# Strassen's algorithm, one level, in the last product of a fused attention, mixture and channel-mixing kernel

## The chip, the cores and the metric

One core of a Trainium2 chip runs the whole program in one launch. The metric is device time in microseconds. The core has five engines with a queue of instructions each: TensorE (matmuls, with weight loads beside them), VectorE, ScalarE, GpSimd and SyncE, which here only issues DMAs.

## The reference

Three layers follow one another, on 8 sequences of 576 tokens (4608 in all), in float32.

- Linear attention with 8 heads of 64: features exp(p) and exp(-p) of the projected queries and keys, a key-value sum per head, a division.
- A mixture of four causal attention experts, the two best per token weighted by a softmax.
- A channel-mixing layer:

```
xk = mu_k * x + (1 - mu_k) * x_prev          # x_prev: the token before
xr = mu_r * x + (1 - mu_r) * x_prev
k  = max(xk @ w_k, 0)                        # 512 -> 1024
v  = (k * k) @ w_v                           # 1024 -> 512   <- the last product
r  = sigmoid(xr @ w_r)
out = r * v
```

## The kernel before, in words

A float32 product is made of three matmuls of float32r parts: every operand is split into a high part and a low part (`split`: the high part is a rounding copy, the low part a subtraction), and high x high, high x low and low x high are added in one PSUM bank.

The program is written as streams of small steps (Python generators) that `weave` mixes by their costs: each step gives a cost, and the stream with the least accumulated cost over its rate is asked next. `skewed` does the same within a stream: a task is a list of stages, and in one step the later stages of older tasks come before the earlier stages of newer ones. A number that each stream gives (its `ahead`) moves the priority of its instructions back: -1000 means as if they had been written 1000 places later. The scheduler then puts each engine's queue in order from priorities and from what it takes to be ready.

The streams are: `favors` (linear attention), `moe1` (the mixture), `compose` and `decodes` (the channel-mixing weights come as 64-bit numbers and are turned into float32 on VectorE and GpSimd), `gates_keys` (tiles `rk`, `z`, `kd`: xr @ w_r and xk @ w_k, in units of six matmuls; results go to DRAM) and `moe2` (tile `vacc`: the last product). `gates_keys` fills TensorE's gaps in the attention part. When `moe1` is done its memory is given up, `late` is set, and a second `weave` mixes what is left of `gates_keys` with `moe2`. There `gates_keys` starts with a credit of 17000 against it.

`moe2` works on six chunks of 768 tokens, each as two halves (`par`, even and odd tokens) of 384. For each half four pieces `kx` of 2 x 384 columns are loaded from `kd` and squared by two ScalarE passes (Relu, Square; L777, L778), split by VectorE into a slot of `XT` (L99, L100) and multiplied with w_v (`wvh2`, `wvl2`, in SBUF as high and low parts): 8 blocks of 128 rows x 4 output blocks x 3 matmuls into four banks. Then VectorE multiplies each bank with the gate `zs` (L802) and the rows of `out` are stored. The first two pieces of the first chunk are made before the phase changes; the others need the memory that `moe1` gives up. The weights w_v are decoded in 16 steps of 256 columns, written to DRAM (`wd`), and read back and split once `favors` is done.

Of the kernel before, what the change touches and what calls it, by code (L numbers as in the profile page):

```python
# [6 lines left out]
F32 = mybir.dt.float32  # L7
# [6 lines left out]
P = 128  # L14
# [62 lines left out]
def fused_kernel(ctx: ExitStack, tc: tile.TileContext, qT, kT, vx, wphi, wq, wk, wvg, wo, mu, w64, ident, cmask, tri, out):  # L77
# [9 lines left out]
    wd = [dram.tile([P, 256], F32, name=f'wd{i}') for i in range(NW)]  # L87
# [37 lines left out]
    pQ = ctx.enter_context(tc.tile_pool(name='pQ', bufs=1, side='right'))  # L125
# [514 lines left out]
    def favors():  # L640
# [16 lines left out]
        wv2.extend(pW.tile([P, 8, DM], F32R, name=n) for n in ('wvh2', 'wvl2'))  # L657
        for f in range(8):
            s_ = pW.tile([P, 768], F32, name='wst2', tag='wst2', bufs=2)[:, :512]
            for j in range(2):  # L660
                nc.sync.dma_start(s_[:, j * 256:(j + 1) * 256], wd[24 + 2 * f + j])
            split(wv2[0][:, f], wv2[1][:, f], s_, 'a', nc.gpsimd)
            yield 2000
    wv2 = []
# [85 lines left out]
    def moe2():  # L750

        def chunk(c, par, os):
            t0 = c * CH
            d = {}
            m = 2 * c + par

            def gate(g):

                def ld():
                    d['z', g] = late['pB'].tile([P, 2, HC], F32, name='zs', tag='zs', bufs=4)  # L760
                    nc.sync.dma_start(d['z', g], kd[c][:, 2 * g:2 * g + 2, par])

                def go():
                    nc.scalar.activation(d['z', g], d['z', g], AF.Sigmoid)
                return [(lambda: 'pB' in late, ld), None, go]

            def kt_(p):

                def ld():
                    if 4 * m + p < 2:  # L770
                        d['s', p] = late['pW'].tile([P, 2 * HC], F32, name='kx', tag='wst2', bufs=2).rearrange('p (u t) -> p u t', u=2)
                    else:
                        d['s', p] = late['pB'].tile([P, 2, HC], F32, name='kx', tag='kx', bufs=6)
                    nc.sync.dma_start(d['s', p], kd[c][:, 4 + 2 * p:6 + 2 * p, par])

                def ev():
                    nc.scalar.activation(d['s', p], d['s', p], AF.Relu)  # L777
                    nc.scalar.activation(d['s', p], d['s', p], AF.Square)  # L778
                    n = (4 * m + p) % 6
                    h_, l_ = (XT[:, (6 * i + n) * 768:(6 * i + n + 1) * 768].rearrange('p (u t) -> p u t', u=2) for i in range(2))  # L780
                    split(h_, l_, d['s', p])
                    d['k', p] = (h_, l_)

                def vmm(i):

                    def go():
                        f = 2 * p + i
                        if f == 0:
                            d['v'] = [late['psB'].tile([P, 512], F32, name='vacc', tag=f'va{dt}')[:, :HC] for dt in range(4)]
                        for dt in range(4):  # L790
                            cs = slice(P * dt, P * dt + P)
                            mm3(d['v'][dt], [(wv2[0][:, f, cs], wv2[1][:, f, cs], *(x[:, i] for x in d['k', p]))], first=f == 0, last=f == 7)
                        return 2070
                    return go

                def fin():
                    if p < 3:
                        return
                    for dt in range(4):
                        if par == 0:  # L800
                            os[dt] = late['pB'].tile([P, CH], F32, name='o', tag='o', bufs=6)
                        nc.vector.tensor_mul(os[dt].rearrange('p (t two) -> p two t', two=2)[:, par], d['v'][dt], d['z', dt // 2][:, dt % 2])  # L802
                        if par:
                            nc.sync.dma_start(out[P * dt:P * dt + P, t0:t0 + CH], os[dt])
                return [(lambda: done.get(c, 0) == NB and B - 1 in read and len(wv2) == 2 and (4 * m + p < 2 or 'pB' in late), ld), None, None, ev, None, (lambda: 'pB' in late, vmm(0)), vmm(1), fin]
            return ([gate(g) for g in range(2)], [kt_(p) for p in range(4)])
        tasks = []
        for c in range(NC_):
            os = {}
            for par in range(2):  # L810
                g, ks = chunk(c, par, os)
                tasks += ks + g
        return skewed(tasks)
# [60 lines left out]
```

## Time and profile before

| | us |
|---|---|
| median of three timed runs | 1287.28 (1287.24 to 1290.59) |
| profiled execution | 1288.14 |
| its span | 1286.3 |
| TensorE busy | 1241.5 (97%) |
| VectorE busy | 877.7 (68%) |
| ScalarE busy | 733.0 (57%) |
| GpSimd busy | 412.6 (32%) |

The span runs from the first to the last instruction of the profiled execution; the profiled execution's own time lies 1.8 us above it. Busy time of TensorE counts overlapping matmuls once. The chain that ended last is TensorE's for 80% of the span.

### The profile page before, as it was taken

How to read it: one execution, taken by the hardware profiler on the slowest of the kernel's cores; microseconds unless marked ns; L12 is line 12 of the kernel's file. 1: busy time of each engine (PE TensorE's matmuls, PEld its weight loads, DVE VectorE, ACT ScalarE, POOL GpSimd, SP SyncE). 2: the span in 40 equal slices, each digit the busy share in tenths (PEclk: the TensorE clock that was granted, in tenths of full speed). 3: DMA queues.
4: the chain of work that ended last, by engine and by line, in shares of the span. 5: the costliest groups of instructions: out<-in, count | busy, mean ns of one | idle time of the engine just before them, and what ended most of it. 6: DMA issues, size and time to landing. Idle time of an engine off the chain costs nothing.

```text
span 1286.3 us, 26695 instructions
## 1 busy us (share of the span) xinstructions
PE 1241.5 (97%) x9152; PEld 1201.2 (93%) x9152; DVE 877.7 (68%) x2476; ACT 733.0 (57%) x1836; POOL 412.6 (32%) x570
## 2 busy tenths in 40 slices
PE   8999999999999999999999999879999989999998
PEld 7999989999999999999999999868988989999998
DVE  6766988788977877876788778546677464443441
ACT  5655767678767665665766565645445474333330
POOL 5532566455633323452444343322112100000000
PEclk9999999999999999999999999999999999999999
DMA  6323125322236444455344434766959887988741
GB/s 189 92 75 100 61 81 164 110 73 75 96 99 190 128 116 133 135 167 182 106 138 138 119 103 141 221 192 199 297 179 278 280 287 242 292 287 285 247 146 50
DMA packets 175127, 208.78 MB, mean 162 GB/s; under 512 B 20497, under 2 KB 160145, under 8 KB 174993
## 3 DMA queue, kind: packets, MB, share of 16 engines
q1 hardware_dynamic: 96656, 136.28, 32.6%
q10 hardware_dynamic: 78336, 70.80, 19.3%
q8 instruction: 74, 1.21, 0.4%
q14 instruction: 61, 0.49, 0.1%
HBM read 143.58 MB, written 63.44 MB: 161 GB/s over the span
## 4 chain that ended last, share of the span: by engine, by line
PE 80%; DVE 7%; DMA 5%; ACT 4%; POOL 2%; issue 1%; ACTq 0%; POOLq 0%; DVEq 0%; SPq 0%
PE rk L117 15%; PE vacc L117 14%; PE kv L327 10%; PE num L365 8%; PE qk L117 6%; PE vp L117 4%; PE yp L580 3%; PE at L545 3%; PE pj L275 3%; PE pj L276 2%; PE pj L277 2%; PE fo L117 2%; PE tq L349 2%; PE sc L507 2%; PE sc L508 2%
## 5 line engine op out<-in xcount | busy, mean ns | idle before, releaser
L117 PE MATMUL vacc<-XT,wvh 128*128 128x384 f32 x768 | 198.8, 336 | 3.9 <-DVE o L802 3.5
L100 POOL TENSOR_TENSOR lo<-raw,hi 128x256 fp32r<-128x256 f32 (+1 forms) x160 | 109.7, 688 | 213.7 <-ACT hi L97 203.3
L538 POOL TENSOR_SCALAR a<-a,sv,gw 128x128 f32<-128x128 f32 (+4 forms) x160 | 107.5, 674 | 213.9 <-DVE sv L532 76.1
L117 PEld LDWEIGHTS vacc<-XT,wvh 128*128 128x128 f32 x768 | 139.7, 189 | 4.6 <-DVE o L802 3.9
L365 PE MATMUL num<-kvs,ph 128*128 128x65 f32 (+1 forms) x1280 | 143.7, 262 | 0.0
L365 PEld LDWEIGHTS num<-kvs,ph 128*128 128x128 f32 (+1 forms) x1280 | 137.4, 181 | 4.9 <-issue 1.8
L117 PE MATMUL vacc<-XT,wvl 128*128 128x384 f32 x384 | 127.4, 336 | 0.0
L527 ACT ACTIVATE a<-sc,sv 128x128 f32<-128x128 f32 (+2 forms) x192 | 98.4, 514 | 45.6 <-DVE sv L522 16.4
L285 DVE TENSOR_REDUCE m<-pj 128x4 f32<-128x512 f32 (+1 forms) x160 | 100.6, 631 | 29.9 <-PE pj L277 28.2
L698 DVE TENSOR_TENSOR z<-rk,z 128x384 f32<-128x384 f32 x144 | 79.5, 553 | 59.3 <-PE rk L117 42.4
L287 DVE TENSOR_TENSOR pm<-pj,m 128x512 f32<-128x512 f32 (+1 forms) x160 | 100.0, 630 | 2.6 <-ACT ph L311 0.6
L275 PE MATMUL pj<-wph,hi 128*128 128x256 f32 x288 | 92.4, 321 | 5.4 <-ACT hi L97 4.5
L522 DVE TENSOR_REDUCE sv<-sc 128x1 f32<-128x128 f32 (+2 forms) x192 | 88.3, 469 | 7.4 <-PE sc L508 4.2
L777 ACT ACTIVATE kx<-kx 128x768 f32<-128x768 f32 x48 | 40.1, 841 | 78.8 <-DMA kx<-kd 63.8
L277 PE MATMUL pj<-wph,lo 128*128 128x256 f32 x288 | 83.9, 292 | 0.5 <-POOL lo L100 0.5
L99 DVE CAST XT<-kx 128x768 fp32r<-128x768 f32 x48 | 26.9, 560 | 84.0 <-PE vacc L117 70.0
L276 PE MATMUL pj<-wpl,hi 128*128 128x256 f32 x288 | 83.5, 290 | 0.0
L97 ACT ACTIVATE hi<-raw 128x256 fp32r<-128x256 f32 (+1 forms) x160 | 62.2, 392 | 30.2 <-PE pj L276 11.3
L561 ACT ACTIVATE at1h<-at 128x384 fp32r<-128x384 f32 (+3 forms) x128 | 53.6, 419 | 45.1 <-PE at L545 24.4
L545 PE MATMUL at<-idn,a 128*128 128x128 f32 (+2 forms) x480 | 73.1, 261 | 2.7 <-DVE sv L524 2.4
L117 PEld LDWEIGHTS vacc<-XT,wvl 128*128 128x128 f32 x384 | 72.5, 189 | 0.0
L562 DVE TENSOR_TENSOR at1l<-at,at1h 128x384 fp32r<-128x384 f32 (+3 forms) x128 | 59.5, 466 | 17.8 <-ACT at1h L561 14.1
(487 smaller groups left out, 3438.7 us busy)
## 6 DMA issues: line engine op xcount, KB each, us to landing
wt<-wf ACTq DMA_DIRECT2D x216, 256.0 KB, 3.7
kd<-z SPq DMA_DIRECT2D x144, 192.0 KB, 3.6
kx<-kd SPq DMA_DIRECT2D x48, 384.0 KB, 4.4
yd<-yt SPq DMA_DIRECT2D x16, 864.0 KB, 4.9
zs<-kd SPq DMA_DIRECT2D x24, 384.0 KB, 5.3
out_dram<-o SPq DMA_DIRECT2D x24, 384.0 KB, 4.1
raw<-in_kT_dram SPq DMA_DIRECT2D x64, 128.0 KB, 2.1
raw<-in_qT_dram SPq DMA_DIRECT2D x64, 128.0 KB, 2.2
```

The source lines that it names most:

```text
L100: (el or nc.vector).tensor_sub(lo, src, hi.bitcast(F32))
L117: nc.tensor.matmul(ps, a, m, start=first and i == 0, stop=last and i == n - 1)
L275: nc.tensor.matmul(o, hi[:, c], wph, start=True, stop=False)
L276: nc.tensor.matmul(o, hi[:, c], wpl, start=False, stop=False)
L277: nc.tensor.matmul(o, lo[:, c], wph, start=False, stop=True)
L285: nc.vector.tensor_reduce(m[:, :g], ps, axis=AX.X, op=OP.max, apply_absolute_value=True)
L287: nc.vector.tensor_sub(pm[:, :g * P].rearrange('p (g f) -> p g f', f=P), ps, m[:, :g].unsqueeze(2).to_broadcast([P, g, P]))
L327: nc.tensor.matmul(bank[:, r, :], d['kp'][:, r % 2, c0:c0 + P], d['v'][:, i + (lo_ > 0), r // 2, :], start=new and r == 0, stop=end, skip_ ...
L365: nc.tensor.matmul(ps[lo_:hi_, i, j, :], d['qp'][:, hf, c0 + lo_:c0 + hi_], kvs[hp, b][:, r * 65:(r + 1) * 65], start=hf == 0, stop=hf == 1)
L527: nc.scalar.activation(a[:m, k0:k1_], o, AF.Exp, bias=nm[:m, 0:1], scale=1.0, accum_out=sm[:m, n:n + 1])
L538: eng(asc).tensor_scalar(a[:m, :nk], a[:m, :nk], rc[:m], WT[b][:m, i, e:e + 1], op0=OP.mult, op1=OP.mult)
L545: nc.tensor.transpose(ps[:kw, jj * m:jj * m + m], d['a'][:m, jj * P:jj * P + kw], idn[:m, :m])
```

## The change

The last product is taken as a 2 x 2 block product. Rows of k (the 1024 features, two halves of 512), columns of w_v (by interleaved blocks of 64) and the two halves of tokens (even, odd) give blocks; in Winograd's form of Strassen's algorithm seven block products replace eight. Each is 512 features x 256 outputs x 384 tokens: 2 output blocks x 4 feature blocks x 3 matmuls (`mm`).

- Weight sums: each decoding step makes four sums of its 64-column blocks on GpSimd (`cs`) and stores seven block columns in one DRAM tensor (`wc`) with two DMAs. `combo` loads one of the seven weight operands and splits it; four are made before the phase changes, three with the first chunk.
- Key sums: T1 = b12 - b11, T2 = b22 - T1, T3 = b22 - b12 and T4 = b21 - T2 of the squared blocks, on GpSimd, 4 x 384 columns each (`sums`). Blocks are loaded in one DMA of 4 x 384 columns; two of four are squared by ScalarE in two passes, two by VectorE in one.
- Splits: each of the seven key operands is split into one of three slots of `XT`, high part on ScalarE, low part on VectorE (`parts`).
- Output sums: products are added up in six banks (`x`, `y`, `w`, two each); in between, banks are copied out and added (`post`). Gate products are taken on GpSimd (two in each chunk on VectorE; in the last chunk four more on VectorE).
- `first` prepares the first three operands of the first chunk before the phase changes. It reads the four blocks itself; the first chunk loads them again.
- `gates_keys` starts the second `weave` without the 17000, with rate 0.85; its priority in the first is moved back by 400 in place of 1000 once `favors` is done. The memory of `moe1`'s query and key weights is given up with the rest.

```diff
@@ decodes
             hz = (yield from decode(pF, i, dict(tag='pm', bufs=3), 'p'))
-            nc.sync.dma_start(wd[i], hz)
+            a11, a12, a22, a21 = (hz[:, 64 * k:64 * k + 64] for k in range(4))
+            cs = pF.tile([P, 4, 64], F32, name='cs', tag='cs')
+            nc.gpsimd.tensor_add(cs[:, 1], a21, a22)
+            nc.gpsimd.tensor_sub(cs[:, 0], cs[:, 1], a11)
+            nc.gpsimd.tensor_sub(cs[:, 2], a12, cs[:, 0])
+            nc.gpsimd.tensor_sub(cs[:, 3], a11, a21)
+            nc.sync.dma_start(wc[:, 0:3, i - 24], hz[:, :192].rearrange('p (j n) -> p j n', j=3))
+            nc.sync.dma_start(wc[:, 3:7, i - 24], cs)
@@ favors, at its end
+        for j in (0, 1, 3, 4):
+            for k in range(2):
+                combo(j, k, 1, pW, pW, 768, 'wst2', 2)()
+                yield 2000
+    def combo(j, k, n, pool, stage, w, tag, bufs):
...
+        nc.sync.dma_start(s_, wc[:, j, q])
+        def go():
+            split(*(x[:, q] for x in WC[j]), s_, 'a', nc.gpsimd)
...
@@ moe2
+        def square(x, e):
+            if e == 'a':
+                nc.scalar.activation(x, x, AF.Relu)
+                nc.scalar.activation(x, x, AF.Square)
+            else:
+                nc.vector.scalar_tensor_tensor(x, x, 0.0, x, op0=OP.max, op1=OP.mult)
+        def first():
...
+            for i in range(2):
+                t1 = half('b11', i)
+                put(0, i, t1)
+                yield 15000
+                t2 = half('b12', i)
+                nc.vector.tensor_sub(t2, t2, t1)
+                yield 15000
+                t1 = half('b22', i)
+                nc.vector.tensor_sub(t1, t1, t2)
+                put(2, i, t1)
+                yield 15000
+            for i in range(2):
+                put(1, i, half('b21', i))
+                yield 15000
...
+            def sums(j):
+                def go():
+                    if j == 2:
+                        nc.gpsimd.tensor_sub(d['b11'], d['b12'], d['b11'])
+                        d['T1'] = d['b11']
...
+                        nc.gpsimd.tensor_sub(d['T2'], d['b22'], d['T1'])
+                        return 8000 if c == 0 else 0
+                    elif j == 5:
+                        nc.gpsimd.tensor_sub(d['b12'], d['b22'], d['b12'])
+                        d['T3'] = d['b12']
+                    elif j == 6:
+                        nc.gpsimd.tensor_sub(d['b21'], d['b21'], d['T2'])
+                        d['T4'] = d['b21']
+            def parts(j):
+                def go():
+                    if c or j > 2:
+                        split(*slot(7 * c + j), d[ops[j]], 'a')
+            def mm(j):
+                def go():
+                    wh, wl = WC[wts[j]]
+                    h, l = slot(7 * c + j)
+                    bank = 'xyxxxww'[j]
+                    for dp in range(2):
+                        if j in (0, 1, 5):
+                            d[bank, dp] = late['psB'].tile([P, 512], F32, name='vacc', tag=f'{bank}{dp}')[:, :HC]
...
+                        for f in range(4):
+                            for a, m in ((wh, h), (wh, l), (wl, h)):
+                                nc.tensor.matmul(ps, a[:, f, dp], m[:, f], start=j in (0, 1, 5) and n == 0, stop=n == 11, skip_group_check=True)
...
+                    return 4200
+            def post(j):
...
+                    for dp in range(2):
...
+                        if j == 0:
+                            d['z', dp] = tmp('t', 3)
+                            evac('a', d['z', dp], x)
+                        elif j == 1:
+                            nc.vector.tensor_add(out_(dp, 0)[:, 0], y, d['z', dp])
+                        elif j == 2:
+                            d['u2', dp] = tmp('u2', 2)
+                            evac('a', d['u2', dp], x)
+                        elif j == 3:
+                            d['u4', dp] = tmp('u4', 2)
+                            evac('a', d['u4', dp], x)
+                        elif j == 4:
+                            o = out_(dp, 0)[:, 0]
+                            nc.gpsimd.tensor_mul(o, o, g(0, 0))
+                            nc.vector.tensor_mul(out_(dp, 0)[:, 1], x, g(1, 0))
+                            store(dp, 0)
+                        else:
+                            t = tmp('t', 3)
+                            nc.vector.tensor_add(t, w, d['u4' if j == 5 else 'u2', dp])
+                            e = nc.vector if c == NC_ - 1 else nc.gpsimd
+                            e.tensor_mul(out_(dp, 1)[:, 6 - j], t, g(6 - j, 1))
+                            if j == 6:
+                                store(dp, 1)
...
+                fs = [[load(*l), None, None, prep(*l), sums(j), parts(j), None, mm(j), post(j)] for j, l in enumerate((('b11',), ('b21',), ('b12', 'b22')))]
+                fs += [[None, None, None, None, None, both(load('g0', 'g1'), parts(3)), None, both(prep('g0', 'g1'), mm(3)), post(3)]]
+            return fs + [[None, None, None, None, sums(j), parts(j), None, mm(j), post(j)] for j in (4, 5, 6)]
@@ the first and the second weave
-(rk, 2.6, 58.0 * 1000.0, lambda: -1000)
+(rk, 2.6, 58.0 * 1000.0, lambda: -400 if 'favored' in state else -1000)
-    weave(tc, (fs, 0.0, 1.0, lambda: 0), (rk, 17000.0, 1.0, lambda: 0), (m2, 0.0, 1.0, lambda: 0))
+    weave(tc, (fs, 0.0, 1.0, lambda: 0), (rk, 0.0, 0.85, lambda: 0), (m2, 0.0, 1.0, lambda: 0))
```

## Rows read from the trace of the kernel before

**Rows 1.** The page's engines: busy us, share of the span, instructions.

```profile
span 1286.3 us, 26695 instructions
...
PE 1241.5 (97%) x9152; PEld 1201.2 (93%) x9152; DVE 877.7 (68%) x2476; ACT 733.0 (57%) x1836; POOL 412.6 (32%) x570
```

**Rows 2.** Busy time by stretch: length, engines with instructions, granted clock, DMA, GB/s.

```profile
950.00:1000.00 50.00, 44.84 (x282) 41.28 (x282) 35.22 (x112) 24.47 (x72) 11.47 (x17) 1.00 0.86 265
...
1050.00:1100.00 50.00, 50.00 (x291) 50.00 (x290) 22.60 (x36) 23.45 (x31) 0.00 (x0) 1.00 0.72 231
```

**Rows 3.** The chain that ended last: start, us, what.

```profile
1165.16 2.95 PE vacc L117 x17
1168.10 2.08 PE rk L117 x12
...
1215.60 63.28 PE vacc L117 x365
```

**Rows 4.** Groups by line, TensorE, high part of the weights.

```profile
L117 PE MATMUL vacc<-XT,wvh 128*128 128x384 f32 x768 | 198.8, 336 | 3.9 <-DVE o L802 3.5
```

**Rows 5.** Busy time by stretch, the change of phase.

```profile
1026.00:1033.00 7.00, 7.00 (x42) 7.00 (x41) 1.52 (x2) 3.69 (x6) 0.00 (x0) 1.00 1.07 366
1033.00:1037.30 4.30, 0.77 (x6) 0.45 (x4) 3.96 (x7) 4.30 (x7) 0.00 (x0) 1.00 0.99 336
1037.30:1041.00 3.70, 3.70 (x12) 3.70 (x13) 3.70 (x7) 3.64 (x6) 0.00 (x0) 0.54 0.94 298
```

**Rows 6.** Waits of TensorE in 1015 to 1060: in total, times, longest.

```profile
PE vacc L117 <- DVE o L802: 3.5, 1, 3.5
```

**Rows 7.** ScalarE by form: count, busy us, mean ns, idle before.

```profile
L777 ACT ACTIVATE kx<-kx 128x768 f32<-128x768 f32 x48 | 40.1, 841 | 78.8 <-DMA kx<-kd 63.8 <-DMA wt<-wf 8.4 <-DVE XT L100 4.0
...
L104 ACT ACTIVATE z<-rk 128x384 f32<-128x384 f32 x72 | 35.0, 488 | 34.6 <-PE rk L117 16.6 <-DMA yc__15645<-yd 5.4 <-DVE o L802 4.2
```

**Rows 8.** VectorE by form.

```profile
L100 DVE TENSOR_TENSOR XT<-kx,XT 128x768 fp32r<-128x768 f32 x48 | 45.9, 957 | 1.4
...
L99 DVE CAST XT<-kx 128x768 fp32r<-128x768 f32 x48 | 26.9, 560 | 84.0 <-PE vacc L117 70.0 <-ACT kx L778 9.0 <-ACT zs L764 4.8
...
L802 DVE TENSOR_TENSOR o<-vacc,zs 128x384 f32<-128x384 f32 x48 | 25.1, 555 | 29.8 <-PE vacc L117 29.7
...
L100 DVE TENSOR_TENSOR sw<-wof,sw 128x512 fp32r<-128x512 f32 x2 | 1.4, 693 | 0.1
```

**Rows 9.** GpSimd by form.

```profile
L100 POOL TENSOR_TENSOR lo<-raw,hi 128x256 fp32r<-128x256 f32 x128 | 94.7, 742 | 177.8 <-ACT hi L97 170.1 <-issue 2.4 <-PE pj L277 2.2
...
L100 POOL TENSOR_TENSOR lo<-raw,hi 128x128 fp32r<-128x128 f32 x32 | 15.2, 475 | 35.9 <-ACT hi L97 33.2 <-PE pj L277 1.6 <-PE pj L276 0.9
...
L100 POOL TENSOR_TENSOR wvl<-wst,wvh 128x512 fp32r<-128x512 f32 x8 | 10.2, 1280 | 12.7 <-ACT wvh L97 8.5 <-DMA kd<-z 4.1
```

**Rows 10.** Timeline, VectorE and GpSimd: start, us, instruction.

```profile
668.66 0.75 DVE L596 TENSOR_TENSOR dl<-yf 128x576 f32<-128x576 f32 x1
668.87 1.23 POOL L100 TENSOR_TENSOR yt<-yf,yt 128x288 fp32r<-128x288 f32 x1 [0.28 <-ACT yt L97]
...
788.07 0.82 POOL L100 TENSOR_TENSOR yt<-yf,yt 128x288 fp32r<-128x288 f32 x1 [2.54 <-ACT yt L97]
...
13.88 0.90 POOL L100 TENSOR_TENSOR lo<-raw,hi 128x256 fp32r<-128x256 f32 x1 [3.22 <-ACT hi L97]
14.11 1.22 DVE L100 TENSOR_TENSOR wkl<-wst,wkh 128x512 fp32r<-128x512 f32 x1
```

**Rows 11.** VectorE on tile rk from 1010: ns min/median/max, first and last start.

```profile
L698 DVE TENSOR_TENSOR z<-rk,z x43: 550/558/560, 1010.3 to 1215.6; 128x384 f32<-128x384 f32 x43
```

**Rows 12.** Timeline, the end.

```profile
1278.97 2.06 DVE L802 TENSOR_TENSOR o<-vacc,zs 128x384 f32<-128x384 f32 x4 [14.59 <-PE vacc L117]
```

More of the change, by code (lines that the diff above doesn't have):

```diff
@@ L86, in fused_kernel @@
     wpl = base.tile([P, 256], F32R, name='wpl')
-    wd = [dram.tile([P, 256], F32, name=f'wd{i}') for i in range(NW)]
+    wc = dram.tile([P, 7, 16, 64], F32, name='wc')
     yd = [dram.tile([P, 2, 2, 3, HP_], F32, name=f'yd{b}') for b in range(B)]
@@ L124, in fused_kernel @@
     XT = pX.tile([P, 16 * S], F32R, name='XT')
-    pQ = ctx.enter_context(tc.tile_pool(name='pQ', bufs=1, side='right'))
+    pQ = phA.enter_context(tc.tile_pool(name='pQ', bufs=1, side='right'))
     wqh, wql, wkh, wkl = (pQ.tile([P, 2, 4, P], F32R, name=n) for n in ('wqh', 'wql', 'wkh', 'wkl'))
@@ L656, in favors @@
         pW = late['pW'] = ctx.enter_context(tc.tile_pool(name='pW', bufs=1))
[L657 to L664, printed above, removed]
+        for j in (0, 1, 3, 4):
+            for k in range(2):
+                combo(j, k, 1, pW, pW, 768, 'wst2', 2)()
+                yield 2000
+    WC = {}
+    def combo(j, k, n, pool, stage, w, tag, bufs):
+        if k == 0:
+            WC[j] = [pool.tile([P, 16, 64], F32R, name=f'wc{x}{j}') for x in 'hl']
+        q = slice(8 * k, 8 * k + 8 * n)
+        s_ = stage.tile([P, w], F32, name='wst2', tag=tag, bufs=bufs)[:, :512 * n].rearrange('p (q n) -> p q n', n=64)
+        nc.sync.dma_start(s_, wc[:, j, q])
+        def go():
+            split(*(x[:, q] for x in WC[j]), s_, 'a', nc.gpsimd)
+            if k + n == 2:
+                WC[j] = [x.rearrange('p (f d h) n -> p f d (h n)', f=4, d=2) for x in WC[j]]
+        return go
     def load_y(c, y, sl, q):
@@ L750, in moe2 @@
     def moe2():
-        def chunk(c, par, os):
-            t0 = c * CH
-            d = {}
[L755 to L761, printed above, removed]
-                def go():
[L764 to L813, printed above, removed]
+        ops = ('b11', 'b21', 'T2', 'T1', 'b22', 'T3', 'T4')
+        wts = (0, 1, 3, 4, 5, 6, 2)
+        src = {'b11': (0, 0), 'b21': (1, 0), 'b12': (0, 1), 'b22': (1, 1)}
+        def slot(n):
+            return [XT[:, (2 * (n % 3) + x) * 1536:(2 * (n % 3) + x + 1) * 1536].rearrange('p (f t) -> p f t', f=4) for x in range(2)]
@@ new lines, in block, with half, put @@
+        def block(c, s, par, f0, f1):
+            return kd[c][:, 4 + 4 * s + f0:4 + 4 * s + f1, par]
+        def square(x, e):
[5 more added lines that the diff above has]
+        def first():
+            while not (done.get(0, 0) == NB and B - 1 in read and len(WC) == 4):
+                yield None
+            raw = {}
+            for n, (x, par) in enumerate((('b11', slot(0)[0]), ('b12', slot(2)[0]), ('b22', slot(2)[1]), ('b21', slot(1)[0]))):
+                raw[x] = par.bitcast(F32)
+                nc.sync.dma_start(raw[x], block(0, *src[x], 0, 4))
+            yield 100000
+            def half(n, i):
+                t = late['pW'].tile([P, 2, HC], F32, name='k0', tag='wst2', bufs=2)
+                nc.scalar.activation(t, raw[n][:, 2 * i:2 * i + 2], AF.Relu)
+                nc.scalar.activation(t, t, AF.Square)
+                return t
+            def put(n, i, t):
+                split(*(x[:, 2 * i:2 * i + 2] for x in slot(n)), t)
+            for i in range(2):
[12 more added lines that the diff above has]
+                yield 15000
+            while 'pB' not in late:
+                yield None
@@ L814, in fused_kernel, with all_ @@
+        def all_():
+            yield from first()
+            yield from skewed([t for c in range(NC_) for t in chunk(c)])
+        return all_()
     clear_pads()
@@ L819, in fused_kernel @@
         nc.sync.dma_start(dst, src)
-    weave(tc, (fs, 0.0, 99.0 * 1000.0, lambda: -1000 if 'favored' in state else 0), (ms, 0.8, 72.0 * 1000.0, lambda: 0), (compose(), 0.35, 206.0 / 2.15, lambda: -1000), (decodes(24, NW), 2.55, 5.0 * 16 / 1.6, lambda: -1000), (load_moe1(), 0.45, 1000.0, lambda: 0), (rk, 2.6, 58.0 * 1000.0, lambda: -1000), (m2, 4.7, 1e6, lambda: 0), until=ms)
+    weave(tc, (fs, 0.0, 99.0 * 1000.0, lambda: -1000 if 'favored' in state else 0), (ms, 0.8, 72.0 * 1000.0, lambda: 0), (compose(), 0.35, 206.0 / 2.15, lambda: -1000), (decodes(24, NW), 2.55, 5.0 * 16 / 1.6, lambda: -1000), (load_moe1(), 0.45, 1000.0, lambda: 0), (rk, 2.6, 58.0 * 1000.0, lambda: -400 if 'favored' in state else -1000), (m2, 4.7, 1e6, lambda: 0), until=ms)
     phA.close()
```

56 lines of the change are left out of this document (55 added, 1 removed).

## The prediction

> **What bounds the kernel now.** I read the page's table of engines first, then busy time by stage, then the chain that ended last, and only then the durations of single forms. TensorE is busy 1241.5 of 1286.3 us [rows 1], so at most 44.8 us can come from idle time, and the rest only from fewer matmuls. By stage [rows 2], the first 1000 us are attention with the key products as filler: TensorE has gaps there (44.84 of 50 us in 950 to 1000). From 1050 on it is busy in every microsecond until the last matmul; the last product (tile vacc) alternates with the key products (tile rk) until 1215.6 and then runs alone: 365 matmuls in 63.28 us, 173 ns each [rows 3]. That is the pitch; the 336 ns of a single record [rows 4] is its latency. So after 1050 a matmul removed is 173 ns gained, provided the other engines deliver on time: VectorE is busy 22.6, ScalarE 23.5 and GpSimd 0 of the 50 us in 1050 to 1100 [rows 2]. The one weak spot is the change of phase. At 1033 to 1037.3 TensorE is busy 0.77 of 4.3 us while the DMA moves 336 to 366 GB/s, and for the 3.7 us after that the granted clock is 0.54, close to the lower of the two levels [rows 5]. Of that gap 3.5 us are a matmul waiting for VectorE to empty a bank [rows 6].
>
> **Removed: one block product in eight.** Before, a chunk costs 2 x 8 x 4 x 3 = 192 matmuls of 384 columns, six chunks 1152. After, it costs 7 x 2 x 4 x 3 = 168 of the same shape, six chunks 1008. 144 x 173 ns = 24.9 us less [rows 3]. The pitch is that of matmuls with a weight load each, which is what stays, so I allow nothing around it. A block product is now 24 x 173 = 4.15 us, a chunk 29.1 us.
>
> **Added on the feeding engines, per chunk.** The operations are twice as long as before; I extend the rows to 1536 elements. ScalarE: 488 ns for 384, 841 for 768 [rows 7], so 0.92 ns per element and 1.55 us. It has two squared blocks (2 x 2 passes), seven high parts, two gates and six evacuations: 13 x 1.55 + 6 x 0.49 = 23.1 us. VectorE: 693 ns for 512, 957 for 768 [rows 8], so 1.75 us; seven low parts and two one-pass squares are 15.8 us, and eight operations on a bank at 0.555 add 4.4: 20.2 us. GpSimd: 475, 742 and 1280 ns for 128, 256 and 512 elements [rows 9], 2.1 ns per element, so 3.43 us for a key sum and 1.01 us for a product with the gate: 4 x 3.43 + 6 x 1.01 = 19.8 us. Each alone fits under 29.1 us, and easily while key products are still between the block products.
>
> **But VectorE and GpSimd do not run side by side.** At 668.66 VectorE subtracts two SBUF tiles for 0.75 us; the GpSimd operation of 128x288 that starts at 668.87 takes 1.23 us, where the same one at 788.07, with no such neighbour, takes 0.82. At 14.11 it is the other way round: VectorE's 128x512 subtraction takes 1.22 us instead of 0.69 while GpSimd is in an operation begun at 13.88 [rows 8, 10]. The loser waits for about the rest of the winner. All nine long VectorE operations of a chunk read two SBUF tiles, and so do all GpSimd ones: 15.8 + 19.8 = 35.6 us in series, against 29.1 us of TensorE. The Trainium skill says this in "SBUF — State Buffer", section "Who interferes with whom": a VectorE instruction with two SBUF inputs and a GpSimd instruction that reads SBUF hold a shared port for the whole instruction, and the other blocks. By that rule the trace agrees in both directions, and the tail would run at 35.6 us per chunk; by the engines' own sums it would run at 29.1.
>
> What counts is how much of the last product runs without filler. The key products' additions end at 1215.6; 43 of them lie after 1010 [rows 11], two in three units, so some 64 units x 6 x 173 ns = 67 us of filler. If the units keep their pace and end near 1205, TensorE has had 195 - 67 - 4 us for block products, 30 of the 42; if they end at 1160, 19. So 12 to 23 products come after the filler. At 23, what is left of the serial work then is: 12 key sums (41), 18 gate products (18), 20 low parts (35) and 5 squares (9), 103 us against 23 x 4.15 = 95 us, with two products still to come after the last low part: some 12 us late. At 12: four sums, eight gate products, nine to ten low parts and one square, 40 us against 50: nothing late. I take +4 us. The ends are 0 and, without filler for 4.7 chunks, 4.7 x 6.5 = 31 us.
>
> **Added waits between products.** Three times in a chunk a product adds into a bank that has just been copied out (after products 3 and 4 by ScalarE, after product 6 by VectorE). Queued behind the waiting matmul are all later matmuls. The copy of the first half hides behind the 2.07 us of the second half, if it takes its 0.49 us at once; behind the two gates and a high part (3 x 1.55) it comes some 1.9 us late. Before, such a wait shows once, 3.5 us [rows 6]. While key products remain they can stand in between. So 1 us in each of the last three chunks: +3 us; the ends are 0 and 6 x 1.9 = 11 us.
>
> **The first chunk, prepared before the phase ends.** Before, two half blocks were squared and split there; now three operands are (b11, b21 and T2). ScalarE: 16 passes for 4, 12 x 0.84 = 10 us more. VectorE: six splits and four subtractions for two splits, 4 x 1.52 + 4 x 0.96 = 9.9 us more [rows 7, 8]. It falls into the last 65 us, where VectorE is busy 35 of 50 us and the attention chain runs through it [rows 2]. The idle remainder hides most of it: +2 us, ends 0 and 10.
>
> **Start of the new phase.** In place of two half blocks three whole products (12.5 us) are ready, and key products start at once instead of 17 us of credit later. Against this stand 0.79 MB for each of four blocks read a second time, and 1.6 MB of weight sums, some 4.7 MB more at a time when the DMA is already full (366 GB/s [rows 5]): 13 us of it, beside 30 us of products and filler. I leave the gap and its slow clock and add 1.4 us for it. The ends: the gap vanishes (-5.2 us, 3.5 of idle and 1.7 of clock), or 8 us more.
>
> **Edits with no cost in the sum.** Four small GpSimd operations in each of 16 decodings (64 elements, 0.34 us by rows 9) are 22 us on an engine that is busy 412.6 us in all [rows 1]; bare of cover, each decoding would hold a low part of the projections up 1.4 us, a few us in all. The two DMAs that store them, in 256-byte pieces on SP's queue, have hundreds of us until they are read. The lower handicap of the key products (-400 for -1000) changes which filler stands where in 800 to 1010; its gaps are worth some us either way, 0 in the sum, ends -6 and +6. The end: after the last matmul an addition and a product follow in place of one product [rows 12], +0.6 us.
>
> **Sum.** 1288.1 (profiled execution) - 24.9 + 4 + 3 + 2 + 1.4 + 0.6 = 1274.2. That execution was 0.9 us above the median of the three timed runs, so about 1273.
>
> **Rivals.**
> - *The whole gain and the gaps too.* Filler lasts to the end, the copies are on time, and three ready products with an earlier filler close the gap: 1287.3 - 24.9 - 5.2 + 0.6 = 1258, with a few us of waiting 1260. For it: each engine is under 80% even without filler. Against: the serial 35.6 us, and a DMA at its limit just then. 0.15.
> - *The shared port sets the tail.* The key products end early because they no longer start late; then 3.3 chunks run at 35.6 us: +21.5, and with the other terms 1287.3 - 24.9 + 21.5 + 3 = 1287. For it: rows 10. Against: the key products came once per 2.5 us or slower before, and buffers let the sums run a chunk ahead. 0.09.
> - *Slower: the chain of key sums is not covered.* In each chunk T1, T2, the high part and the low part of T2 follow one another: 3.43 + 3.43 + 1.55 + 1.75 = 10.2 us, and TensorE's operand slots hold only three products. The written order gives from the squares to the use of T2 four products, 16.6 us, of which squares and GpSimd's gate products take some 6. If VectorE's operations come between the sums, 5 us or more of it are bare in each chunk. It decides from 24.9 / 6 = 4.1 us per chunk; at 6 us the time is 1287.3 - 24.9 + 36 = 1298. For it: the margin is about nil without filler. Against: with filler a step takes nearly twice as long. 0.11.
> - *The freed time is not TensorE's to give.* If the DMA or the pace of the key products set the end, fewer matmuls only make idle time. After the last key unit the last chunk still needs some 43 us up to its last matmul (22 to T2, five products), so units that end at 1215 as now would allow 1265 and no less; only units that end later bind. Within the forecast's range.
>
> **How the numbers follow.** Forecast 0.65, the others as given. A difference under 0.3% (1283.4 to 1291.1) can't be told from none. The forecast reaches from 1264 to 1283; with part of the first rival and the lower part of the others the range is 1260 to 1287. Faster: 0.15 + 0.65 and a little of the second rival, 0.82. Same: most of the second rival, 0.07. Slower: 0.11.
>
> **What would show it.** 1008 vacc matmuls at 173 ns after the change of phase; after the last key product, gaps in TensorE that end with ScalarE or VectorE, no more than a few us per chunk; GpSimd sums clearly over 3.43 us and VectorE's long subtractions over 1.75 where they overlap. It is wrong if those stretch nothing, if TensorE idles over 4 us per chunk, or if the stage before 1010 moves by over 10 us.

## The result, and the profile after

The changed kernel took 1307.05 us (median of 6 runs, 1302.85 to 1310.23); the kernel before, beside it on the same chip, 1288.88. The ratio is 1.0145 with a 95% interval of 1.0126 to 1.0163. It is slower by 1.45%; the forecast was 1273, faster, and the time lies outside its range. The profiled execution took 1303.78 us with a span of 1302.0, 15.7 us more than that of before.

The page of after, engines and the two groups that matter:

```profile
PE 1232.5 (95%) x9008; PEld 1186.1 (91%) x9008; DVE 966.5 (74%) x2451; ACT 770.2 (59%) x1846; POOL 604.2 (46%) x693
...
L886 PE MATMUL vacc<-XT,wch 128*128 128x384 f32 x672 | 179.8, 346 | 22.8 <-DVE XT L100 11.4
...
L100 DVE TENSOR_TENSOR XT<-kx,XT 128x1536 fp32r<-128x1536 f32 x39 | 110.2, 2833 | 38.0 <-ACT XT L97 36.6
```

The 144 matmuls are gone (9008 for 9152 in [rows 1]), yet TensorE is busy only 9 us less. The last group is the first sign of the cause: VectorE's low parts last 2833 ns in the mean where 1.75 us was forecast. The second is TensorE's idle time in front of L886: of its 22.8 us 11.4 end with exactly this line. Before, the last product waited for VectorE once for long, 3.5 us, for the emptying of a bank [rows 6].

Busy time by stretch in after (length, PE, PEld, DVE, ACT, POOL, granted clock, DMA share, GB/s):

```profile
950.00:1000.00 50.00, 41.92 (x234) 38.65 (x232) 33.25 (x89) 28.28 (x68) 8.34 (x11) 0.90 0.90 292
...
1036.00:1050.00 14.00, 14.00 (x83) 14.00 (x82) 3.43 (x4) 2.98 (x5) 2.23 (x2) 1.00 0.79 271
1050.00:1070.00 20.00, 11.59 (x46) 10.26 (x46) 17.06 (x8) 14.45 (x15) 17.72 (x4) 0.66 1.03 361
1070.00:1100.00 30.00, 29.23 (x169) 28.91 (x168) 20.81 (x16) 16.15 (x15) 30.00 (x11) 1.00 0.93 304
1100.00:1211.30 111.30, 106.79 (x604) 104.16 (x603) 83.02 (x67) 62.57 (x64) 67.08 (x26) 1.00 0.78 260
1211.31:1298.00 86.69, 73.86 (x390) 71.97 (x389) 61.25 (x42) 36.60 (x34) 56.01 (x20) 0.90 0.37 124
```

Before, the same kind of row showed no gap from 1041 to 1215.6 and nearly none after it:

```profile
1026.00:1041.00 15.00, 11.47 (x57) 11.15 (x56) 9.18 (x15) 11.62 (x17) 0.00 (x0) 0.89 1.02 341
1041.00:1100.00 59.00, 59.00 (x343) 59.00 (x342) 28.82 (x45) 32.38 (x43) 0.00 (x0) 1.00 0.75 243
1100.00:1215.60 115.60, 115.60 (x668) 115.60 (x668) 50.69 (x83) 41.12 (x56) 0.00 (x0) 1.00 0.87 283
1215.60:1281.00 65.40, 64.83 (x374) 64.51 (x373) 23.92 (x37) 13.56 (x16) 0.00 (x0) 1.00 0.32 101
```

So after has three losses: the start of the phase, scattered ones up to the last key product at 1211.3, and the end without filler. For the last stretch the chain of waits shows what TensorE waits for; its lines are start, us, what:

```profile
1225.42 1.38 ACT XT L97
...
1226.88 4.46 DVE XT L100
...
1231.72 4.56 DVE XT L100
...
1236.33 16.96 PE vacc L886 x81
```

In [rows 3] one unbroken run of 365 matmuls stood here. Now the chain runs through two of VectorE's subtractions, each 2.7 to 2.8 us longer than 1.75.

**A measure for the comparisons.** By *tail loss* I mean the time from the first to the last matmul of tile vacc, less the number of TensorE's matmuls in it at 0.1733 us, the pitch of [rows 3]. It holds idle time and slow clock together. Before: 270.1 us, 1524 matmuls, 6.0 us lost. After: 261.1 us, 1284 matmuls, 38.5 lost, 25.9 of them idle and 12.6 at a lower clock. The difference of the two executions is then: 25.0 less in matmuls, 32.6 more tail loss, 9.3 from a last product that starts late (1035.9 for 1010.0, of which 16.6 are key products done earlier), 1.3 less behind the last matmul. Together +15.6; measured +15.7. Some expectations below have 38.6 for 38.5 and 9.6 for 9.3.

A tail loss is that of one profiled execution, and the executions of one kernel lay 2 to 16 us apart: a few us between two tail losses say little. The profiled execution of e6, for instance, was the slowest of its five, 5.4 us above their median.

### The profile page after: what moved, and what is told of

Read it like the earlier page. It is cut to its first block, busy times and chain, and to the rows that moved or that the text cites. A ratio compares the mean times of both kernels' runs of the same rounds, so it can differ in the third digit from the quotient of the medians.

```text
span 1302.0 us, 26511 instructions
## 1 busy us (share of the span) xinstructions
PE 1232.5 (95%) x9008; PEld 1186.1 (91%) x9008; DVE 966.5 (74%) x2451; ACT 770.2 (59%) x1846; POOL 604.2 (46%) x693
## 4 chain that ended last, share of the span: by engine, by line
PE 68%; DVE 9%; DMA 7%; ACT 6%; POOL 5%; issue 3%; ACTq 1%; SPq 0%; POOLq 0%; DVEq 0%
PE rk L117 12%; PE kv L334 10%; PE num L372 8%; PE vacc L886 6%; PE qk L117 6%; PE vp L117 4%; PE yp L587 3%; PE at L552 3%; PE pj L282 3%; DMA kd<-z 2%; PE pj L283 2%; PE pj L284 2%; PE fo L117 2%; DVE XT L100 2%; PE tq L356 2%
## 5 line engine op out<-in xcount | busy, mean ns | idle before, releaser
L886 PE MATMUL vacc<-XT,wch 128*128 128x384 f32 x672 | 179.8, 346 | 22.8 <-DVE XT L100 11.4
L886 PEld LDWEIGHTS vacc<-XT,wch 128*128 128x128 f32 x672 | 125.8, 195 | 27.4 <-DVE XT L100 13.1
L100 DVE TENSOR_TENSOR XT<-kx,XT 128x1536 fp32r<-128x1536 f32 x39 | 110.2, 2833 | 38.0 <-ACT XT L97 36.6
L886 PE MATMUL vacc<-XT,wcl 128*128 128x384 f32 x336 | 115.2, 344 | 0.8 <-POOL wcl L100 0.8
L97 ACT ACTIVATE hi<-raw 128x256 fp32r<-128x256 f32 (+1 forms) x160 | 62.2, 392 | 32.6 <-PE pj L283 11.4
L97 ACT ACTIVATE XT<-kx 128x1536 fp32r<-128x1536 f32 x39 | 57.5, 1483 | 39.2 <-PE vacc L886 16.9
L514 PE MATMUL sc<-k,qs 128*128 128x128 f32 (+2 forms) x192 | 65.6, 350 | 5.2 <-ACT a L534 5.2
```

The costliest lines, as they stand in the source:

```text
L886: nc.tensor.matmul(ps, a[:, f, dp], m[:, f], start=j in (0, 1, 5) and n == 0, stop=n == 11, skip_group_check=True)
```

## The experiments

Times are ratios to the kernel before in the same job, with 95% intervals.

**Sums left out, and sums made for nobody.** e1 takes the key sums away (their products then use other operands). e2 makes the same four sums on GpSimd into a tile that nobody reads: GpSimd as busy as in after, no chain from sums to products.

```
 if j == 2:
-    nc.gpsimd.tensor_sub(d['b11'], d['b12'], d['b11'])
...
+    d['T1'], d['T2'], d['T3'], d['T4'] = (d[n] for n in ('b11', 'b22', 'b12', 'b21'))
+    nc.gpsimd.tensor_sub(d['S'], d['b12'], d['b11'])     # e2 alone, and three more
```

> The four key sums of each chunk are left out (each product takes an unsummed block in place of T1 to T4), so GpSimd has only the gate products in the tail, 6 instead of 20 us of work per chunk. Theory P (VectorE's long operations and GpSimd's block each other): VectorE's low parts and squares fall back to a median of 1.75 us, TensorE's lost time in the tail (38.6 us of the 261.5 after 1035.8: 25.9 idle, 12.7 by a slow clock) falls to 5 to 12, the time to 1270 to 1280. Rival C (no blocking needed: the sums are simply a long chain before products 3, 4, 6 and 7): the same. Rival F (the loss is in the stage before, where the first vacc matmul comes at 1035.8 in place of 1009.8, and in the second reading of blocks): the time stays above 1295.

> GpSimd makes four sums per chunk of the same size at the same places, into a tile that nobody reads; the products take unsummed blocks. So GpSimd's work and its reads of SBUF stay, and the chain through the sums is gone. Theory P: VectorE's low parts still stretch (median over 2.2 us, up to 5 us), and most of the loss stays: 1292 to 1305. Rival C: the loss goes as if the sums were left out: 1270 to 1280. Rival F: as in the first run, above 1295.

e1: 1291.0 us, 1.0022 (1.0001 to 1.0043), tail loss 27.6; 1270 to 1280 and 5 to 12 were expected. e2: 1311.7 us, 1.0187 (1.0152 to 1.0222), tail loss 47.5, as slow as after and above the expected range. VectorE's low parts in e1 and then in e2, and GpSimd's sums in e2 (count, ns min/median/max, first and last start):

```profile
L100 DVE TENSOR_TENSOR XT<-kx,XT x39: 1742/1759/2831, 1048.8 to 1274.7; 128x1536 fp32r<-128x1536 f32 x39
```

```profile
L100 DVE TENSOR_TENSOR XT<-kx,XT x39: 1742/2092/5115, 1049.8 to 1295.3; 128x1536 fp32r<-128x1536 f32 x39
...
L855 POOL TENSOR_TENSOR ks<-kx x6: 3499/3669/5020, 1053.4 to 1250.0; 128x1536 f32<-128x1536 f32 x6
L856 POOL TENSOR_TENSOR ks<-kx x6: 3422/4949/5027, 1057.0 to 1255.5; 128x1536 f32<-128x1536 f32 x6
```

With nobody waiting for the sums the time stays lost, and the two engines stretch each other as in after. So the loss does not need the chain of sums; the sums' work beside VectorE's is enough. Its price, from e1 to e2 in the same job, is 20.7 us of the medians and 20 us of tail loss. (e2 also keeps one buffer more than e1. e6 below keeps it too and is fast.) The 27.6 us that e1 still loses are another matter: its low parts are short, and more than half of it lies before 1100.

**The sums on VectorE, the gate products on VectorE, then both.** e3 moves the four sums (`nc.gpsimd.tensor_sub` to `nc.vector.tensor_sub`), e5 only the products with the gate (`nc.vector.tensor_mul(o, o, g(0, 0))`, `e = nc.vector`). e6 does both and makes the low parts of the three late weight operands on VectorE too, so that GpSimd has nothing to do after the change of phase.

```
-                        nc.gpsimd.tensor_sub(d['T2'], d['b22'], d['T1'])
+                        nc.vector.tensor_sub(d['T2'], d['b22'], d['T1'])
...
-    split(*(x[:, q] for x in WC[j]), s_, 'a', nc.gpsimd)
+    split(*(x[:, q] for x in WC[j]), s_, 'a', nc.gpsimd if n == 1 else nc.vector)
```

> The key sums on VectorE, 1.75 us each instead of 3.5 on GpSimd: VectorE's own work rises to 27.2 us per chunk of 29.1. Theory P: nothing but gate products is left on GpSimd to block, VectorE's long operations return to 1.75 us, the tail loses 8 to 16 us in place of 38.6: 1274 to 1284. Rival C: the chain is shorter by half (3.5 for 6.9 us before T2), but VectorE's queue is nearly full: 1280 to 1295. Rival F: no change, 1300 or more.

> Only the gate products move from GpSimd to VectorE (0.55 us each there, with one input from a bank for half of them). Theory P (VectorE's and GpSimd's SBUF reads exclude each other): GpSimd loses 32 operations of 1.0 to 2.5 us (58 us in the trace of the change), the key sums stay, so a smaller part of the loss goes than with the sums moved (17 us): 1296 to 1303. Rival C (the key sums' chain): no gain, 1304 to 1310.

> Key sums, gate products and the low parts of the three late weight operands all on VectorE; GpSimd has nothing to do after the change of phase. Theory P: VectorE's low parts take 1.75 us at the most, not only in the median; the 3.9 us that single operations still took at 1056 to 1064 with the key sums on VectorE go, and with them some of the 12 us of gap there: 1276 to 1284. Against it: VectorE's own work is then 30.4 us per chunk of 29.1, so it may set the end once key products run out: 1284 to 1290, with VectorE full in the last 60 us.

e3: 1289.6 us, 1.0018 (1.0000 to 1.0035), tail loss 26.2. That lies in the range of rival C, not of theory P; what speaks against C is e2. e5: 1306.3 us, 1.0159 (1.0127 to 1.0191), tail loss 47.1: no gain, against the expectation. TensorE's longest waits in e5 (in total, times, longest):

```profile
PE vacc L886 <- DVE XT L100: 13.4, 6, 4.0
PE rk L117 <- DVE z L715: 11.5, 5, 4.3
```

In e6 the same two come to 0.8 and 1.8 us. So the sums, twenty-four of 3.5 us, are enough to keep VectorE from its work; beside them GpSimd has only the low parts of the late weights to make in e5. e6: 1280.33 us, **0.994 (0.9919 to 0.9961)**, tail loss 18.0: as theory P expected, and faster than before and than after, though VectorE has some 10 us per chunk more to do (4 x 1.75 + 6 x 0.55), in place of GpSimd's 20. Its low parts all take their 1.75 us, and the stretches change thus:

```profile
L100 DVE TENSOR_TENSOR XT<-kx,XT x39: 1743/1752/1761, 1057.5 to 1268.8; 128x1536 fp32r<-128x1536 f32 x39
```

```profile
1050.00:1070.00 20.00, 11.14 (x47) 10.02 (x46) 17.21 (x14) 14.95 (x14) 0.00 (x0) 0.68 1.06 380
1070.00:1100.00 30.00, 29.11 (x165) 28.79 (x165) 27.03 (x28) 17.37 (x18) 0.00 (x0) 0.98 0.99 327
1100.00:1211.30 111.30, 111.30 (x644) 111.30 (x643) 85.64 (x93) 65.16 (x65) 0.00 (x0) 1.00 0.80 268
1225.50:1280.00 54.50, 50.37 (x286) 49.09 (x284) 39.56 (x45) 28.57 (x28) 0.00 (x0) 1.00 0.40 140
```

By length less matmuls x 0.1733: 1100 to 1211.3 lost 6.6 us in after (604 matmuls) and nothing in e6 (644); from the last key product to the last matmul after lost 18.3 (390 matmuls in 85.9 us), e6 4.1 (286 in 53.7, its key products ending later). The start, 1050 to 1070, lost 12 in both, so the sums on GpSimd are not its cause.

**The handicap of the key products.** e4 puts only -1000 back into after, e7 into e6. e10 and e11 start from e6 with T1 made and split first in chunk 0, raise the rate of the key products (1.4 for 0.85), and take -1000 and -700.

```
-(rk, 2.6, 58.0 * 1000.0, lambda: -400 if 'favored' in state else -1000)
+(rk, 2.6, 58.0 * 1000.0, lambda: -1000)
```

> Only the key products' handicap in the first weave is put back to -1000 after the linear attention. Rival F in the form that -400 lets the key products push the attention's end back: the first vacc matmul returns to 1010 to 1020 and the time falls by 5 to 12 us, to 1292 to 1300. Theory P alone: the attention may end earlier, but the key products that are done less before it come back later, so the time changes by less than 4 us and the tail's lost time stays over 30 us.

> As the one before, with the key products' handicap in the first weave put back to -1000. Rival F (the stage before costs 9.6 us because -400 lets key products go ahead of the attention): with GpSimd out of the tail the 5 us of earlier start are no longer lost again, and more key products are left as filler for the start of the phase: 4 to 10 us below the one before, 1270 to 1278. If the stage before is worth nothing: within 3 us of the one before.

> As the one before, with the handicap -1000 in the first weave and rate 1.4 for the key products in the second. With -1000 the stage before lost 2 us instead of 12, but the key products ended at 1240 instead of 1225 and the last chunk waited for them (11 us idle and a slow clock at 1240 to 1260). If that end was late because of the rate 0.85, it comes back to 1225 and the time is 1264 to 1272; if the pace is set by their own DMAs and buffers, the end stays late: 1280 to 1290.

> The same with -700: between the two above. The first vacc matmul at 1020 to 1030, 1266 to 1280.

e4: 1.0144 (1.0101 to 1.0187); the stage before is only 4.1 us late instead of 9.3, but the tail loss is 48.5. e7: 1293.6 us, 1.0049 (1.0031 to 1.0068), 36.6; e10: 1299.8 us, 1.0094 (1.0077 to 1.0111), 41.2; e11: 1288.1 us, 1.0008 (0.9981 to 1.0034), 29.8. These three missed their expectations. In e7 the last addition of a key product starts at 1240.5 (1225.5 in e6), and then:

```profile
1200.00:1240.00 40.00, 40.00 (x233) 40.00 (x232) 20.24 (x27) 12.74 (x15) 0.00 (x0) 1.00 0.73 228
1240.00:1260.00 20.00, 8.50 (x31) 7.03 (x29) 10.23 (x8) 13.33 (x10) 0.00 (x0) 0.66 0.43 152
```

Full until 1240, 8.5 of 20 us after: the last chunk waits for the last key products, and its last matmul comes some 47 us behind them. The higher rate didn't bring them earlier (1250.0 in e10). So -1000 gives up at the end what it gains before 1010 (e4), or more (e7).

**The start of the phase.** All from e6. e8 neither loads nor splits the three late weight operands (their products use others). e9 makes T1 and its parts first in chunk 0. e12 lets products 4 to 6 of chunk 0 take operands that lie in the slots already (`if c or j > 2:` to `if c or j > 5:`; their results are other ones).

> As the second of this group, but the three late weight operands are neither loaded nor split; products 5 to 7 take the first three operands again. Theory S (the start of the phase is bound by what it loads: 3.1 MB of blocks a second time and 1.6 MB of weights): the gap at 1050 to 1065 and its slow clock shrink by 4 to 8 us, and the time by as much. If the gap is made by the order of the work on VectorE and ScalarE and not by bytes: less than 3 us.

> On the kernel with GpSimd idle after the change of phase (1280.3): in the first chunk VectorE makes T1 and its low part before T2 and T3, and the late weights and b21 come after them on ScalarE. Theory O (what is left of the gap at 1050 to 1070, 9 us idle and some 5 us by the slow clock, is the order of work behind T1, not bytes): product 4 starts about 5 us earlier, the time falls by 5 to 8 us, to 1272 to 1276. Theory S (bytes loaded at the start): less than 3 us.

> On the kernel with GpSimd idle after the change of phase (1280.3): in the first chunk products 4 to 6 take the operands that lie in the three slots already (no high and low parts for them); all loads, squares and sums stay, and so do their bytes. Theory R (the start of the phase waits for the chain behind the release of memory: load, squares, T1, its parts; three prepared products do not cover it): with 12.5 us of matmuls more at hand the gap at 1050 to 1070 goes, 9 us idle and some 5 us of slow clock: 1266 to 1272. Theory S (the bytes at the start set the time, through the key products' own DMAs): the idle time moves to another place and the time stays within 4 us of 1280.

e8: 0.9975 (0.9951 to 0.9999), tail loss 18.3. e9: 0.9988 (0.9966 to 1.0009), 20.6. e12: 0.9982 (0.9964 to 1.0001), 22.2. None gained on e6's 0.994: what theory S forecast for e8, O for e9 and R for e12 did not come. In e12 the gap of 1050 to 1070 is gone and another one, of 10.8 us, stands at 1082 to 1094. ScalarE there (ACTq is the issue of a DMA from its queue):

```profile
1077.51 1.47 ACT L97 ACTIVATE XT<-kx 128x1536 fp32r<-128x1536 f32 x1
1082.89 0.53 ACTq L761 DMA_DIRECT2D wt<-wf  x1
1083.51 7.50 ACTq L690 DMA_DIRECT2D yc__15583<-yd  x4
1091.05 0.53 ACTq L761 DMA_DIRECT2D wt<-wf  x1
1091.62 1.48 ACT L97 ACTIVATE XT<-kx 128x1536 fp32r<-128x1536 f32 x1 [12.64 <-DMA yc__15583<-yd]
```

It works on nothing for 12.6 us; the loads of the key products, which it issues itself, stand in front of the next split, and the copy of a bank (`t`) that TensorE waits for comes behind that split:

```profile
PE vacc L886 <- ACT t L104: 12.4, 2, 10.8
```

So e13 (on e6) and e14 (on e12) issue these loads from GpSimd's queue, e15 and e16 from SyncE's, from the change of phase on:

```
-                nc.scalar.dma_start(w.bitcast(F32), wf[u][:, :, sl])
+                (nc.sync if 'late' in state else nc.scalar).dma_start(w.bitcast(F32), wf[u][:, :, sl])
```

> The version with GpSimd idle after the change of phase, with the loads of the key products' weights and activations issued from GpSimd's queue instead of ScalarE's from the change of phase on. Same bytes, same arithmetic. Theory Q (ScalarE stands behind these issues): ScalarE's splits come on time, the idle time of TensorE in 1050 to 1070 falls from 9 us to under 4 and the time from 1280 to about 1273 to 1276, ratio to before 0.989 to 0.991. Theory S (the DMA's load and the work per operand set the start): the gap stays within 2 us, 1279 to 1283, ratio 0.993 to 0.997.

> The version in which products 4 to 6 of the first chunk take operands that lie in the slots already (so their results are not the reference's), with the same loads issued from GpSimd's queue. Theory Q: the gap of 10.8 us at 1080 to 1094 goes, no stretch of 14 us loses more than 3 us to idling, about 1272 to 1276, ratio 0.987 to 0.991. Theory S: the gap only moves again, 1281 to 1286, ratio 0.996 to 1.0.

> The version with GpSimd idle after the change of phase, the key products' loads issued from SyncE's queue from the change of phase on. Theory Q (ScalarE standing behind its own issues costs the tail time): 1270 to 1277, ratio 0.987 to 0.992. Theory S (bytes and feeding work at the start): 1278 to 1284, ratio 0.993 to 0.998, with the gap at 1050 to 1070 unchanged. If SyncE's stores of key products hold the loads up behind them, key products end later than 1231 and the time is above 1285.

> The same on the version in which products 4 to 6 of the first chunk take operands that lie in the slots already (their results are not the reference's). Theory Q: both gaps gone, 1262 to 1272, ratio 0.981 to 0.988. Theory S: the gap moves to another place, 1278 to 1286.

e13: 1.0312 (1.028 to 1.0343), e14: 1.032 (1.0294 to 1.0346), far slower, which neither theory expected. GpSimd's queue in e13:

```profile
1087.86 0.73 POOL L690 DMA_DIRECT2D yc__15573<-yd  x1 [4.85 <-DMA wt<-wf]
1094.31 0.72 POOL L690 DMA_DIRECT2D yc__15578<-yd  x1 [5.73 <-issue]
1100.78 0.73 POOL L690 DMA_DIRECT2D yc__15578<-yd  x1 [5.74 <-issue]
1103.99 0.73 POOL L690 DMA_DIRECT2D yc__15578<-yd  x1 [2.49 <-issue]
```

It brings one load forth every 3 to 6.5 us, and the key products wait for them:

```profile
PE rk L117 <- DMA wt<-wf: 17.5, 8, 4.6
```

On the question itself these two runs say little. e15: 1281.3 us, 0.9957 (0.9932 to 0.9981), tail loss 19.5, the gap at 1050 to 1070 unchanged (9.9 of 20 us busy): no gain, as theory S had it. e16: 1278.9 us, 0.9922 (0.9898 to 0.9946), 13.2. Its time is theory S's too, slower than theory Q's 1262 to 1272. TensorE where e12 had its gap, first in e12, then in e16:

```profile
1080.00:1094.00 14.00, 3.18 (x17) 2.77 (x16) 9.77 (x8) 2.38 (x4) 0.00 (x0) 0.78 1.06 386
```

```profile
1060.00:1070.00 10.00, 8.32 (x48) 7.94 (x47) 9.97 (x8) 7.73 (x8) 0.00 (x0) 1.00 1.05 383
1070.00:1080.00 10.00, 10.00 (x60) 10.00 (x59) 8.46 (x9) 7.72 (x7) 0.00 (x0) 1.00 1.07 373
1080.00:1094.00 14.00, 13.12 (x71) 11.90 (x69) 12.58 (x16) 9.94 (x10) 0.00 (x0) 1.00 0.96 304
```

So there were two things behind one another. The gap at 1050 to 1070 is the making of products 4 to 6's operands: VectorE is busy 17.2 of the 20 us in e6, and the gap goes when they are ready (e12, e14, e16) and for no other edit. The gap at 1082 to 1094, which shows only then, is ScalarE behind its own loads, and it goes with another queue (from e12 to e16 the tail loss falls from 22.2 to 13.2, the ratio from 0.9982 to 0.9922). The DMA is as full in e16 at 1060 to 1080 (373 to 383 GB/s) with TensorE busy, so its load by itself doesn't make these two gaps.

But a third gap stands behind them: at 1094 to 1110 of e16 TensorE is busy 11.7 of 16 us, with one wait of 4.4 us for a low part, and what makes it was not tested. With its last product starting 3.5 us later as well, e16 can't be told from e6 in time (0.9922 and 0.994, intervals that overlap). So both causes are seen in the traces, and no run shows a gain in time over e6 from removing them. The best kernel with the whole arithmetic remains e6 (e15 can't be told from it).

## Why the prediction was wrong

**The matmuls: right.** 1008 of them, at the same pitch where nothing interrupts them (78 in 13.53 us from 1211.3); 25.0 us for 24.9.

**"I take +4 us" for the shared port: the step that failed.** The mechanism was named from [rows 10] and the ends were 0 to 31; the size was some 21 us (tail loss 38.5 in after, 18.0 in e6; 20.7 by the medians of e1 and e2), and from after to e6 in ratios 2% or 26 us. The durations of a single operation were right: 1.75 us for a low part and 1.01 for a gate product where nothing stands beside them, 3.50 for a sum (3.43 forecast). In after they are these:

```profile
L100 DVE TENSOR_TENSOR XT<-kx,XT x39: 1745/2347/5044, 1054.6 to 1286.8; 128x1536 fp32r<-128x1536 f32 x39
...
L853 POOL TENSOR_TENSOR kx<-kx x6: 3502/3836/5126, 1052.2 to 1257.2; 128x1536 f32<-128x1536 f32 x6
...
L859 POOL TENSOR_TENSOR kx<-kx x6: 3508/4984/5031, 1061.2 to 1267.6; 128x1536 f32<-128x1536 f32 x6
...
L926 POOL TENSOR_TENSOR o<-t,zs x20: 1012/2468/2545, 1091.4 to 1272.5; 128x384 f32<-128x384 f32 x20
```

The maxima are one operation and nearly all of the other: 5.04 = 1.75 + 3.3 of a sum's 3.5; 5.0 = 3.5 + 1.5 of a low part's 1.75; 2.47 = 1.01 + 1.46. By the rule of the Trainium skill in "SBUF — State Buffer", section "Who interferes with whom", the two contend for a port that is locked and not shared, so the one that comes second is blocked until the other's instruction ends; the trace agrees with these maxima. In the time line of after one sees them take turns:

```profile
1264.10 3.51 POOL L856 TENSOR_TENSOR kx<-kx 128x1536 f32<-128x1536 f32 x1
1266.13 3.09 DVE L100 TENSOR_TENSOR XT<-kx,XT 128x1536 fp32r<-128x1536 f32 x1 [2.67 <-ACT XT L97]
1267.57 4.98 POOL L859 TENSOR_TENSOR kx<-kx 128x1536 f32<-128x1536 f32 x1
...
1270.92 5.72 DVE L100 TENSOR_TENSOR XT<-kx,XT 128x1536 fp32r<-128x1536 f32 x2 [0.76 <-ACT XT L97]
```

What was wrong in the working was to treat the port as a budget of time per chunk (35.6 us of serial work against the TensorE time of the stretch). Its case of 23 products comes to 103 + 8.3 - 95 = 16 us late by its own terms, where it has 12. But even so 16 products without filler, which is what there were (390 matmuls at 24), cost only about 4 to 6 us between its two cases. Measured, that stretch lost 18.3 us, 14.2 more than e6's. A budget supposes that work is done ahead; in the time line it wasn't. All four waits of the stretch, 12.2 us, stand before product 3 (T2's) of the last two chunks. In the first of them T1's low part, at 1226.88, stands behind T2's sum, and T2's own low part, next in VectorE's queue at 1231.72, behind T3's sum, which is wanted only three products later; each is 2.7 to 2.8 us late. T2's sum itself is stretched to 5.00 us.

So this stretch is lost where the rival "chain of key sums" put it, with every step of the chain open to the port. What the chain would cost with sums of 3.5 us that nothing stretches was not tested: e3 and e6 keep the chain but shorten its sums to 1.75 us, and in e6 T2's products wait 0.8 us or less.

And the working set the cost to nothing while filler remains; there it was 6.6 us. The slower clock makes the gaps dearer: it was granted at 0.90 from 1211 to 1298, where e6's row from 1225.5 shows 1.00.

**Waits for a bank, +3: right in size, by luck.** TensorE's waits in 1035 to 1300 of after:

```profile
PE vacc L886 <- DVE XT L100: 11.4, 4, 4.3
PE vacc L886 <- ACT XT L97: 8.3, 3, 3.1
PE vacc L886 <- ACT t L104: 3.1, 3, 1.2
```

The third line is these waits, 3.1 us (2.7 in e6). But they lie at 1102, 1110 and 1203, beside key products, which were to hide them; in the chunks without filler, where they were forecast, there is none.

**The start, +1.4: too low.** 12 us are lost in 1050 to 1070 of after (46 matmuls), 5.1 in 1026 to 1041 before (57): +6.9, near the upper end given. The step counted the ready products and the DMA; it did not count the work between the landing of a block and the product. That this work makes the gap is shown on e6, by e12 and e16; after has the same gap in the same place.

**The first chunk's preparation, +2, and -400 for -1000, 0: too low together.** The last product begins 9.3 us later than the key products done ahead explain. How this divides is open. e4, with -1000, is 4.1 us late, but the lateness varies about as much where nothing before the phase was changed: 4.1 to 15.3 us over the thirteen kernels with -400, 2.0 to 5.2 over the three with -1000.

**The end, +0.6:** 1.3 us shorter instead.

**Together.** Between the sum, 1274.2, and the profiled execution, 1303.8, lie 29.6 us. Some 16.5 are the port (20.5 for 4), 7.3 the stage before (9.3 for 2), 5.5 the start (6.9 for 1.4); the end gives 1.9 back, and 2.2 are not accounted for.

**The signs.** 1008 matmuls and stretched operations showed. Of the signs of being wrong one came: TensorE idled 25.9 us in the tail, 4.3 per chunk, where over 4 was named. The stage before moved by 9.3 us, just under the 10 named.

**The rivals.** "The shared port sets the tail" had the mechanism right, and its +21.5 is close to the 20.5 measured. That is partly luck: it put the loss into 3.3 chunks without filler, there were 2.3, and 6.6 us were lost beside filler. Its time, 1287, lacked the late stage and most of the start. "The chain of key sums" had the sign and, in the last two chunks, the place right (6.6 and 5.6 us bare, where it had 5 or more). It needs no stretching, and e2 shows the loss without any chain, mostly in front of other products: the chain is one way the port's cost reaches TensorE, not what makes it. "The freed time is not TensorE's to give" did not bind in after, whose last matmul is 86 us behind the last key product. In e7 it did, and its 43 us were measured as 47; e4 and e10, whose key products end at 1250, fit it (51 and 46).

## What to carry to other kernels

Two engines that exclude each other are not a budget to be summed over a stage: ask for each operation that something waits for, which longer operation can stand in front of it, and charge that whole length each time there is no slack. Moving work to an idle engine can cost more than leaving it on a busy one: here GpSimd's 20 us of work per chunk, given back to VectorE as 10 us, made the kernel 26 us faster. And an engine's own queue counts as a resource: in e12 the loads that ScalarE issues stood in front of its arithmetic for 12.6 us.

## What was not expected of the hardware

- A sum of 128x1536 on GpSimd (3.50 us) and a low part on VectorE (1.75 us) reach 5.1 and 5.04 us when they meet, in both directions, so a single meeting costs up to 3.3 us on an engine whose operation takes half of that.
- DMA loads issued from GpSimd's queue came 3 to 6.5 us apart in e13 (0.73 us of work each), those from SyncE's queue did not hold the kernel up: 1.0312 against 0.9957 for the same loads.
- Left open: the 13.2 us that e16 still loses, its third gap among them, and how the 9.3 us of the stage before divide.
